# The load of lam in an attention and feed-forward kernel, issued from the Pool queue

## Chip, core and metric

The kernel runs on one core of one Trainium2 chip. The metric is the device time of one execution in microseconds. Before the change it is 221.66 us, the median of twelve runs, which lie between 219.85 and 223.47.

The engines are named as in the profile: PE is the matrix engine (TensorE), ACT is ScalarE, DVE is VectorE, POOL is GpSimd, and SP is SyncE, which here only issues transfers. A transfer (DMA) is issued by SP, ACT or POOL; each of these has a queue of its own for it, and all transfers are carried out by the same 16 DMA engines of the core.

## The reference

For 4 batches, 8 heads, 768 positions and a head size of 64, a linear attention with a decay `lam` for each head is followed by a feed-forward layer. The attention works in blocks of 64 positions:

```python
Dmask = np.where(rel >= 0, lam[:, None, None] ** rel[None, :, :], 0.0)
lam_pow = lam[:, None, None] ** (pos[None, :, None] + 1)
for b in range(nb):
    intra = einsum('bhic,bhjc->bhij', qb, kb) * Dmask[None]
    intra = einsum('bhij,bhjd->bhid', intra, vb)
    inter = einsum('bhid,bhde->bhie', qb * lam_pow[None], kv_state)
    out[:, :, sl] = intra + inter
    kv_state = lam_block * kv_state + einsum('bhsd,bhse->bhde', kb * rev_pow, vb)
```

Its output, as 3072 tokens of 512 values, goes through `x @ w_in` (512 by 2048), a smooth ReLU, which is 0 below -1, h above 1 and (h + 1)^2 / 4 between, and `g @ w_out` (2048 by 512). `lam` has eight values, one for each head; every other number of the attention is scaled by powers of them.

## The kernel before

**Tiles.** The 3072 tokens are 24 blocks of 128 (c = 0 to 23, six of them to a batch). Four blocks are a stage of 512 tokens for the feed-forward layer, so that there are six stages. The matrices of the layer, `w_in_sb` and `w_out_sb`, are loaded once in four pieces each, by POOL (L188, L192), and kept.

**How lam is used.** Instead of a decay in each product, q and k are scaled by tables of powers of lam before anything else. `lam_b` (L106) is a tile of 128 rows in each of which the eight values stand; it is loaded by one transfer that reads the same 32 bytes for each row (L107). ACT takes its logarithm (`ln_lam`, L144), DVE multiplies it with the positions (`arg`, L146), and ACT makes three tables by exponentials: `tab_q` (L149), `tab_p` (L151) and `tab_k` (L154). The positions come from two iotas on POOL (L113, L114) and a copy on ACT (L140).

**A block.** q of two blocks is loaded as `x0f` (L585), k as `x1f` and v as `x2f` (L597); for the first two blocks k and v come together as `raw` (L592). All these loads are issued by SP, in an order that the planner sets. The scaled q is `qs` (L296), on DVE or POOL; the scaled k is `ks` (L287). PE transposes both through PSUM (`py`, L332, and `pt`, L325), ACT copies q's result to `qT` (L338), DVE copies k's to `kT` (L342) or `kbd` (L335). PE multiplies them (`ps`), DVE masks the scores (`sc`, L405 to L410), PE makes the state (`pu`) and the output (`po`), and ACT copies the output to `xT` (L458). From `xT` on the feed-forward layer takes over: PE with `w_in_sb` into `ph` (L470), ACT and DVE for the smooth ReLU (L479 to L500), PE with `w_out_sb` into `py` (L518), ACT to the output tile (L523), SP to memory.

**Setup on POOL.** Before its first `qs`, POOL makes an identity for the transposes, the two iotas, the causal masks (L116 to L126) and clears two of the four tiles `vi` (L138). DVE clears other tiles (L134 to L142) in the same time, and ACT loads its function table (L105).

**Order.** The setup stands in program order on each engine. All that follows is set by a planner, `run_plan` (L217): every operation has an engine, an estimated time, the operations it needs and a time when it is due, and a small simulation of five engines and the transfers decides the order on each engine. Its only guess at the start of the transfers is `FIRST_BYTE` (L212), the time in ns at which the first load is taken to begin.

**First loads.** SP issues the first q (c = 0 and 1), raw k, raw v, k for c = 2, the second q, v for c = 2, k and v for c = 3. POOL issues the first piece of `w_in` after k for c = 2 has landed, and the other three after the second q has been scaled.

Of the kernel before, what the change touches and what calls it, by code (L numbers as in the profile page):

```python
# [23 lines left out]
def kernel(  # L24
# [16 lines left out]
    nc = tc.nc  # L41
# [62 lines left out]

    nc.scalar.preload_act_table_set("natural_log_exp_and_others")  # L105
    lam_b = const.tile([128, H], F32)  # L106
    nc.scalar.dma_start(out=lam_b, in_=lam.partition_broadcast(128))  # L107


    ident = const.tile([128, 128], BF16)  # L110
# [7 lines left out]
        out=causal, in_=causal, compare_op=AX.is_ge, fill=0.0,  # L118
# [3 lines left out]
    for e in range(2):  # L122
        for rows, base in ((slice(0, 128), 128 - e), (slice(0, 64), -e)):
            nc.gpsimd.affine_select(
                out=causal2[rows, e], in_=causal2[rows, e], compare_op=AX.is_ge, fill=0.0,
# [15 lines left out]
    for t in kbd[2:] + ubd[1:]:  # L141
# [10 lines left out]
                         in_=arg[:, 1].rearrange("p (e m) h -> p e (m h)", e=2)[:, :, :2 * H], func=AF.Exp, scale=-1.0)  # L152
# [56 lines left out]
        ops.append(OPS[key])  # L209

    MMS, FETCH = {"s": 8, "o": 12}, 1300
    FIRST_BYTE = 2950  # L212
    LDD, QXD, KXD, STD = 20000, 7000, 7000, 3000
    ON_POOL, ON_DVE = (1,), ((0, 1),)
    W_AFTER = {1: ("cq", 1, 1), 2: ("cq", 1, 1)}
# [1 line left out]
    def run_plan(free):  # L217
# [21 lines left out]
        for x in topo:  # L239
            if not x.needs:  # L240
                ready[x.eng].append((0, x))
        out_seq, xfer, dma_free, fetched = [], [0] * RING, FIRST_BYTE, 0
        while len(out_seq) < len(ops):
# [548 lines left out]
```

## Time and profile before

| | |
|---|---|
| median of twelve runs | 221.66 us |
| the profiled execution's own time | 222.71 us |
| its span on the core | 221.0 us |
| granted clock of PE | 1.00 |
| first matmul starts | 9.41 us |
| lam: issued, from ACT's queue; ln_lam starts | 0.84 us; 6.78 us |
| first q: issued by SP; first qs starts on DVE, on POOL | 0.81 us; 7.76 us, 7.80 us |
| raw k: issued by SP; first ks starts on DVE, on POOL | 1.32 us; 9.56 us, 9.60 us |
| first w_in piece issued by POOL | 12.40 us |
| last matmul ends | about 217.9 us |

The page gives for each engine the time in which it was busy, the chain of work that ended last, and groups of like instructions. Times in the views count from the start of the span. A releaser, what ended an engine's idle time, is inferred from semaphore events. For a transfer the profile gives the time of its issue on the queue and the time from issue to landing, and for each stretch the number of packets that each queue moved: q1 is SP's, q10 is ACT's, q0 is POOL's.

### The profile page before, as it was taken

To read this page: it belongs to the slowest core of one execution; us is meant where nothing else is said; L and a number is where in the kernel's file an instruction comes from. 1 tells how busy PE (TensorE), PEld (TensorE's weight loads), DVE (VectorE), ACT (ScalarE), POOL (GpSimd) and SP (SyncE) were. 2 spreads that over 40 slices of the span, in tenths; PEclk is the share of its full clock that TensorE was granted. 3 is DMA by queue.
4 is the path that set the end of the run, shared out by engine and by line. 5 is a ranking of instruction groups with operands and counts; after the bars stand their busy time and mean duration, and the time that the engine had idled before them with its cause. 6 is when DMAs were issued, how large, how long until landed. Compare 5 with 4: busy or idle time off the path is not lost.

```text
span 221.0 us, 4453 instructions
## 1 busy us (share of the span) xinstructions
PE 203.3 (92%) x1776; PEld 132.8 (60%) x1800; DVE 141.6 (64%) x216; ACT 123.0 (56%) x220; POOL 64.1 (29%) x71
## 2 busy tenths in 40 slices
PE   0189889999999999999999999999999999999994
PEld 0158778686847977777667776654545444444443
DVE  5275859689581888897876866740697745554301
ACT  2247668646646767486757667645665544445030
POOL 8563066217534162733240730332100000000000
PEclk9999999999999999999999999999999999999999
DMA  3999999999999898959999926998985211110122
GB/s 91 254 224 203 178 219 167 177 204 204 176 201 214 177 223 164 249 106 232 195 245 160 260 72 140 203 207 184 293 138 173 47 47 50 47 47 0 50 95 95
DMA packets 96116, 35.42 MB, mean 160 GB/s; under 512 B 78560, under 2 KB 93152, under 8 KB 96096
## 3 DMA queue, kind: packets, MB, share of 16 engines
q1 hardware_dynamic: 91728, 30.94, 66.8%
q0 software_dynamic: 4224, 4.19, 12.0%
q8 instruction: 14, 0.23, 0.4%
q14 instruction: 6, 0.05, 0.1%
q10 hardware_dynamic: 144, 0.00, 0.0%
HBM read 27.27 MB, written 6.29 MB: 152 GB/s over the span
## 4 chain that ended last, share of the span: by engine, by line
PE 90%; DMA 3%; ACT 2%; DVE 2%; issue 1%; POOL 1%; DVEq 0%
PE ph L470 38%; PE py L518 36%; PE ps L398 3%; DMA lam_b<-in_lam_dram 3%; PE po L428 3%; PE pu L369 2%; PE py L512 1%; PE po L425 1%; PE py L332 1%; PE pt L325 1%; PE po L420 1%; ACT xT L458 1%; PE po L446 1%; PE po L417 1%; POOL qs L296 1%
## 5 line engine op out<-in xcount | busy, mean ns | idle before, releaser
L470 PE MATMUL ph<-xT,w_in_sb 128*128 128x256 bf16 (+2 forms) x763 | 95.7, 272 | 1.7 <-ACT xT L458 1.2
L479 ACT ACTIVATE r<-ph,one 128x512 bf16<-128x512 f32 x96 | 65.9, 688 | 48.7 <-PE ph L470 31.8
L518 PE MATMUL py<-w_out_sb,gT 128*128 128x512 bf16 x349 | 86.5, 379 | 1.2 <-issue 0.3
L470 PEld LDWEIGHTS <-w_in_sb 128*128 128x128 bf16 x768 | 63.3, 98 | 24.7 <-issue 1.9
L518 PEld LDWEIGHTS <-gT 128*128 128x128 bf16 x368 | 34.8, 98 | 34.9
L489 DVE TENSOR_SCALAR t<-r 128x1024 bf16<-128x1024 bf16 x48 | 25.1, 524 | 36.6 <-ACT r L479 36.6
L500 DVE TENSOR_TENSOR gT<-w,t 128x1024 bf16<-128x1024 bf16 x48 | 39.6, 825 | 1.5
L495 DVE TENSOR_TENSOR w<-r,t 128x1024 bf16<-128x1024 bf16 x48 | 38.3, 798 | 1.5
L287 POOL TENSOR_TENSOR ks<-x1f,tab_k 128x512 bf16<-128x512 f32 x20 | 23.0, 1149 | 32.0 <-DMA x1f<-in_k_dram 15.6
L296 POOL TENSOR_TENSOR qs<-x0f,tab_q 128x512 bf16<-128x512 f32 x15 | 19.0, 1282 | 17.5 <-PE ph L470 6.0
L523 ACT COPY osb<-py 128x512 f32<-128x512 f32 x23 | 13.5, 585 | 17.9 <-PE py L518 16.6
L373 ACT CAST ubd<-pu 64x256 bf16<-64x256 f32 x40 | 14.6, 364 | 7.4 <-PE pu L369 3.7
L294 POOL TENSOR_TENSOR qs<-x0f,tab_qn 128x512 bf16<-128x512 f32 x8 | 9.7, 1212 | 27.3 <-DMA x0f<-in_q_dram 22.6
L410 DVE TENSOR_TENSOR sc<-ps,causal 128x512 bf16<-128x512 f32 x12 | 8.3, 689 | 9.6 <-PE pt L398 9.6
L458 ACT CAST xT<-po 128x512 bf16<-128x512 f32 x15 | 8.8, 584 | 8.3 <-PE po L428 5.1
L332 PE MATMUL py<-ident,qs 128*128 128x128 bf16 x16 | 2.4, 306 | 10.1 <-POOL qs L296 9.4
L428 PE MATMUL po<-sc,vi 128*128 128x128 bf16 x112 | 10.5, 219 | 0.0
L428 PEld LDWEIGHTS <-vi 128*128 128x128 bf16 x112 | 8.4, 98 | 1.0
L332 PEld LDWEIGHTS <-qs 128*128 128x128 bf16 x24 | 2.1, 121 | 11.0 <-POOL qs L296 9.4
L425 PE MATMUL po<-qT,ubd 128*128 128x128 bf16 x48 | 8.7, 219 | 0.0
L410 DVE TENSOR_TENSOR sc<-ps,causal_n 128x512 bf16<-128x512 f32 x8 | 5.5, 686 | 4.8 <-PE pt L398 4.8
L320 ACT CAST vi<-x2f 128x512 bf16<-128x512 f32 x14 | 8.5, 616 | 0.0
(84 smaller groups left out, 138.7 us busy)
## 6 DMA issues: line engine op xcount, KB each, us to landing
out_dram<-osb SPq DMA_DIRECT2D x23, 256.0 KB, 2.6
x1f<-in_k_dram SPq DMA_DIRECT2D x22, 256.0 KB, 4.9
x2f<-in_v_dram SPq DMA_DIRECT2D x22, 256.0 KB, 4.8
x0f<-in_q_dram SPq DMA_DIRECT2D x8, 512.0 KB, 5.0
w_in_sb<-in_moe_w_in_dram POOLq DMA_DIRECT2D x4, 512.0 KB, 8.7
w_out_sb<-in_moe_w_out_dram POOLq DMA_DIRECT2D x4, 512.0 KB, 9.0
x0f<-in_q_dram SPq DMA_DIRECT2D x8, 256.0 KB, 4.0
raw<-in_k_dram SPq DMA_DIRECT2D x1, 512.0 KB, 8.1
```

The costliest lines, as they stand in the source:

```text
L287: eng.tensor_tensor(ks[c], qkv_ld[c, 1], _bc(tab, 2, D), op=AX.mult)
L296: eng.tensor_tensor(qs[m, e], qkv_ld[m, 0][:, :, e], _bc(tab_q[:, e, m % (NCB // 2), :], 2, D), op=AX.mult)
L373: nc.scalar.copy(out=ubd[c % NUB][HD[hi], :, HD[hi]], in_=pu[0][HD[hi], :, HD[hi]])
L410: nc.vector.tensor_tensor(sc_sb[c][:, g], pst[c, g], _bc(causal if c < DX else causal_n, 1, HP), op=AX.mult)
L428: nc.tensor.matmul(po[:, hp], lhsT=vi[c % NV][:, hp, hi].rearrange("p a d -> p (a d)"), rhs=sc_sb[c][:, hi, hp, :], start=(cb == 0 and hi ...
L470: nc.tensor.matmul(ph[:, j * m:(j + 1) * m], lhsT=w_in_sb[:, ko, (ni + j) * 128:(ni + j + 1) * 128], rhs=xT[s][:, ko, tok], start=(ko == 0 ...
L479: nc.scalar.activation(out=o, in_=x, func=AF.Relu, bias=one[:, 0:1])
L489: nc.vector.tensor_scalar(t, r, 0.5, 1.0, op0=AX.mult, op1=AX.min)
L495: nc.vector.tensor_tensor(w, r, t, op=AX.subtract)
L500: nc.vector.tensor_tensor(gT[s][:, f - RW * n:f, tok].rearrange("p (a b) m -> p a b m", a=RW), w.rearrange("p a (b m) -> p a b m", m=m), t ...
L518: nc.tensor.matmul(py_t[s, ms], lhsT=gT[s][:, ko, ms * 128:(ms + 1) * 128], rhs=w_out_sb[:, ko, :], start=(ko == 0), stop=(ko == FO - 1))
L523: nc.scalar.copy(out=osb[s, ms], in_=py_t[s, ms])
```

## The change

One line issues lam's load from POOL instead of ACT, at the same place in the program, and the planner's guess at the first load's start is 500 ns lower.

```diff
     nc.scalar.preload_act_table_set("natural_log_exp_and_others")
     lam_b = const.tile([128, H], F32)
-    nc.scalar.dma_start(out=lam_b, in_=lam.partition_broadcast(128))
+    nc.gpsimd.dma_start(out=lam_b, in_=lam.partition_broadcast(128))
...
     MMS, FETCH = {"s": 8, "o": 12}, 1300
-    FIRST_BYTE = 2950
+    FIRST_BYTE = 2450
```

## Prediction

> **What bounds the kernel now.** I read the page first: its span, its engine shares and the chain that ended last.
>
> ```profile
> span 221.0 us, 4453 instructions
> PE 203.3 (92%) x1776; PEld 132.8 (60%) x1800; DVE 141.6 (64%) x216; ACT 123.0 (56%) x220; POOL 64.1 (29%) x71
> PE 90%; DMA 3%; ACT 2%; DVE 2%; issue 1%; POOL 1%; DVEq 0%
> ```
>
> TensorE is busy for 203.3 of 221.0 us. The table of busy time by stretch tells where its idle time is (columns: stretch, length, then busy time and instruction count of each engine).
>
> ```profile
> 0.00:9.40 9.40, 0.00 (x0) 0.00 (x0) 4.25 (x11) 2.19 (x6) 6.03 (x18) 1.00 0.68 177
> 9.40:29.30 19.90, 16.56 (x196) 13.69 (x197) 12.06 (x20) 11.59 (x24) 7.21 (x7) 1.00 1.05 193
> 29.30:216.80 187.50, 185.75 (x1565) 118.25 (x1589) 124.44 (x183) 109.19 (x191) 50.90 (x46) 1.00 0.79 158
> ```
>
> Up to 9.40 us TensorE does nothing; then it is 83% busy (16.56 of 19.90); from 29.30 on it idles only 1.75 of 187.50 us. So a shift of the first matmul reaches the end nearly one for one, if the stretch from 9.4 to 29.3 passes it on. The head of the chain, in order of time, is where the change acts (start, length, what).
>
> ```profile
> 0.84 5.92 DMA lam_b<-in_lam_dram
> 6.76 0.02 issue
> 6.78 0.22 ACT ln_lam L144
> ...
> 7.03 0.27 DVE arg L146
> ...
> 7.32 0.24 ACT tab_q L149
> ...
> 7.82 1.54 POOL qs L296
> ...
> 9.41 0.62 PE py L332 x4
> ```
>
> This seems to say that lam's load sets the first matmul. I doubt it. qs needs tab_q, ready at 7.32 + 0.24 = 7.56, and also q's first tile x0f. The view of line L296 shows the wait for x0f as an instruction of its own, ahead of the multiplication; the list of DMA issues gives both landings.
>
> ```profile
> L296 POOLq EVENT_SEMAPHORE  x1: 17/17/17, 7.7 to 7.7; - x1
> x0f<-in_q_dram SPq DMA_DIRECT2D x1, 512.0 KB, 6.8
> lam_b<-in_lam_dram ACTq DMA_DIRECT2D x1, 4.0 KB, 5.9
> ```
>
> x0f is issued at 0.81 and lands 6.8 later, at about 7.6; the wait ends at 7.7 and qs starts at 7.8. For the next cast, ks at L287, the same view has its wait for raw k end at 9.5 and its multiplication start at 9.6, with tables that are two microseconds old by then. The same 0.1 us in both says that x0f's landing, not the tables, released qs. The page infers its releaser; lam is ready some 0.1 us before it is needed. So an earlier lam alone is worth nothing; x0f has to land earlier, or lam later, for the time to move.
>
> **The change, part by part.** Built, both kernels have the same instructions in the same order on every engine except for one row: lam's DMA leaves ScalarE's list and stands in POOL's, after the start barrier and ahead of the identity's memset. So the second edit, FIRST_BYTE 2950 to 2450, moves nothing: 0 us. Semaphore lanes are renumbered. One wait goes (v's load for c = 3 waited for the first q load, landed at 7.6, and issues at 11.92: 0 us); the last w_out load now waits for lam's lane, done some 30 us before: 0 us.
>
> *ScalarE loses an issue* of 0.42 us at 0.84. It ran beside the table load (0.81 to 2.09), and ScalarE then idles 4.5 us until lam: 0 us.
>
> *POOL gains an issue.* The POOL rows of the trace are four w_in issues of 747 to 929 ns, the first being the longest; lam's 4 KB in 128 rows may cost less. I take 0.93. Everything behind it on POOL moves by that: identity, two iotas, two causal masks, two memsets of vi. They end at 5.44 and would end at 6.4; POOL then idles until 7.8 (2.37 us before qs), so it is hidden. Should qs start earlier than 6.4 the cover is gone and each further us costs one. ScalarE's cast of pos_i would start at about 2.4 instead of 2.10, well ahead of lam. Nothing on SP's queue moves in order.
>
> *When does lam land from POOL?* The trace has no small load from there, so bounds. Its issue runs from 0.80 to 1.7. The first w_in issue ended at 13.33 and its queue's first packets came between 14.2 and 14.7, so 0.9 to 1.4 later: lam's first packet at 2.6 to 3.1. From below, w_in(0)'s 528 packets took from there to its landing at 12.40 + 7.5 = 19.9, at most 5.7 us; lam's 144 packets at that rate are 1.6: landing from 4.2 on. From above, lam itself took 6.76 − 2.5 = 4.3 from its first packet on the ScalarE queue: landing by 7.4. I take 5, nearer to the rows of the software queue that it will use. ln, arg and tab_q take 0.80 after it (6.76 to 7.56), so that lam may land up to 6.85 without touching a qs at 7.8. At 5 it costs 0; at 7.4 it costs 0.55.
>
> The Trainium skill, "DMA: Bandwidth & Descriptors", section "Specifications", speaks against the change: it gives about 1 us to the first byte by the GpSimd path and 0.6 by SyncE and ScalarE. By that alone lam would land 0.4 later, at 7.16, and the kernel would lose 0.3 us. No row here shows it.
>
> *What the other loads gain.* This decides. The DMA view by stretch counts packets by queue; q1 is SP's, q10 is lam's.
>
> ```profile
> q1 hardware_dynamic: 164, 0.08, 61.0%
> q10 hardware_dynamic: 4, 0.00, 0.5%
> ...
> q1 hardware_dynamic: 344, 0.18, 48.9%
> q10 hardware_dynamic: 91, 0.00, 3.0%
> ```
>
> The first pair is 2.5 to 3.0 us, the second 3.0 to 4.5. Before lam's packets SP's queue moved 164 per half us and was rising. While 91 of lam's 144 pass, it moves 344 in three halves, 115 each, and the engines are half idle (48.9%). It climbs again to 981 in the three halves from 5.5 to 7.0, with 8 lam packets left. So lam's packets stand where SP's queue falters, and x0f is the load in flight. Had SP's queue kept 164, it would have moved 492: 148 more, which at 164 per half us is 0.45 us. Had it run at 327 from 3.0 to 5.5 it would have moved 1635 instead of 733 (344, and 155 and 234 in the two halves after 4.5): 902 packets, 1.4 us at 327. If lam's packets disturb in the same way from another queue, or the dip is the start of HBM reads and not lam, it is 0. A loss in this term is excluded, since the same 144 packets are served either way. I take 0.45, the rate that the queue had shown by then; ends 0 and 1.4.
>
> *Does the stretch to 29.3 pass it on?* qs, tq, qT and the second tq follow one another; the key transpose at 11.07 needs ks, whose load raw k landed at 9.4 (ks done at 10.25), so 0.45 passes even if raw k stays. Next: ks for c = 2 needs x1f, landed 12.1, used 13.91 (1.8 spare); w_in(0) lands 19.9, used 22.46 (2.5 spare); x2f for c = 3 lands 20.5, used 22.17 (1.6 spare); w_in(1) lands 16.29 + 7.9 = 24.2, used about 25.3 (1.1 spare). So 0.45 passes whole; over 1.1 passes only as far as these loads come earlier too.
>
> **The sum.** ScalarE 0, POOL 0, lam's lateness 0, SP's loads −0.45. Against the profiled execution: span 221.0 − 0.45 = 220.55, and with the 1.71 us around it (222.71 − 221.0) 222.26. That execution is 1.05 above the median of the twelve runs, 221.66, so the median forecast is 221.66 − 0.45 = 221.2. About 0.5%, 1.1 us, is what a measurement of this kernel can tell from no change.
>
> **Rivals.**
> *The transfer is hidden anyway.* The dip belongs to the start of the loads, x0f lands at 7.6 as before: 221.7. For it: 65 packets only in the half us from 2.0 to 2.5, before any of lam's. Against it: the fall after 3.0 comes with lam's packets.
> *The whole dip is lam's.* SP's queue runs on at 327 and x0f lands 1.4 earlier, raw k and the rest with it: 220.3. For it: the recovery follows the end of lam's packets; a 512 KB q load takes a median of 5.0 to land later on, against 6.8 here. Against it: loads before 3.0 were slow without lam, and the tables would have to be ready at 6.2, so lam landed by 5.4.
> *Slower: descriptors made on POOL come late, lam takes x0f's place as the last releaser.* The place is ScalarE's wait at L144; it decides from a landing after 6.85, one for one, since ln, arg, tables, qs and the first matmul queue behind it. Price: like w_in's quickest load, 7.5, landing would be at 8.3, 1.45 late: 223.1; like their median, 8.7, 2.65 late: 224.3. DVE's memsets fill 0.88 to 4.49, beside the issue; would POOL be held until they end, the first packet would come at 5.4 to 5.9 and lam, 1.6 to 4.3 later, at 7.0 to 10.2. Against it: POOL's two memsets of vi, one beside DVE's memsets and one after them, show 944/944/944 ns, so DVE's memsets didn't hold that one; and w_in carries 128 times lam's bytes.
> The Trainium skill, "SBUF — State Buffer", section "SBUF: two separate sides", warns of this: while VectorE runs an operation in a two-port mode, GpSimd can't write descriptors. Memset isn't named there; if it counted, lam would be held as above, and the time be 221.8 to 225.0.
>
> **How the numbers follow.** Chances: forecast 0.40, hidden anyway 0.14, whole dip 0.26, late lam 0.20. The first two lie within 0.5% of before (0.54), the third is faster by over 0.5%, the fourth slower by over 0.5%. The predicted time is the first's, 221.2. Its own range, from 0.55 for a lam at 7.4 to −1.1 for what the spare of w_in(1) passes, is 220.5 to 222.2. The range of 8 in 10 reaches to 220.0, just past the third, and to 223.1, the cheapest end of the fourth.
>
> **What would show it.** Right: lam lands between 4 and 6.5; x0f within 0.2 to 0.8 earlier than 7.6; ScalarE's wait at L144 shrinks and L296 starts on x0f's landing; the first matmul comes at about 9.0 and the idle time after 29.3 stays near 1.75. Wrong: x0f lands at 7.6 as before, and the first matmul stays at 9.4; or L296 waits again for the tables, lam landing after 6.85; or the first matmul moves and TensorE's idle time between 9.4 and 29.3 takes it back, most likely at the second w_in group.

## The result, and the profile after

| | before | after |
|---|---|---|
| median, us | 221.67 (49 runs, 219.85 to 223.47) | 222.56 (12 runs, 222.14 to 223.25) |
| profiled execution, us (its span) | 222.71 (221.0) | 222.24 (220.5) |

The ratio of after to before is 1.0047, with a 95% interval from 1.0026 to 1.0067: so after is slower, by 0.9 us between the medians. The two profiled executions alone would say the opposite, since that of before was a slow one of its kind; this is taken up below. VectorE, ScalarE and POOL run the same instructions in the same order in both traces, but for lam's issue, so the planner's lower guess has moved nothing and the difference is lam's queue.

The start of after in order of time (start, length, engine, line, operation; in brackets the idle time before it and what ended it):

```profile
1.34 0.71 POOL L107 DMA_DIRECT2D lam_b<-in_lam_dram  x1 [0.83 <-POOLq L776]
...
7.21 0.21 ACT L144 ACTIVATE ln_lam<-lam_b 128x8 f32<-128x8 f32 x1 [4.16 <-DMA lam_b<-in_lam_dram]
...
7.75 0.24 ACT L149 ACTIVATE tab_q<-arg 128x48 f32<-128x48 f32 x1 [0.33 <-DVE arg L146]
...
8.02 0.69 DVE L296 TENSOR_TENSOR qs<-x0f,tab_q 128x512 bf16<-128x512 f32 x1 [0.31 <-ACT tab_q L149]
8.07 1.54 POOL L296 TENSOR_TENSOR qs<-x0f,tab_q 128x512 bf16<-128x512 f32 x1 [1.37 <-ACT tab_q L149]
8.63 1.53 DVE L287 TENSOR_TENSOR ks<-raw,tab_p 128x512 bf16<-128x512 f32 x1
...
9.67 0.61 PE L332 MATMUL py<-ident,qs 128*128 128x128 bf16 x4 [9.67 <-POOL qs L296]
```

Its first DMA issues, with microseconds from issue to landing:

```profile
x0f<-in_q_dram SPq DMA_DIRECT2D x1, 512.0 KB, 4.3
raw<-in_k_dram SPq DMA_DIRECT2D x1, 512.0 KB, 6.7
lam_b<-in_lam_dram POOLq DMA_DIRECT2D x1, 4.0 KB, 5.8
```

x0f now lands at 0.81 + 4.3 = 5.1 instead of 7.6. But lam lands at 1.34 + 5.8 = 7.15, and qs starts at 8.02 and 8.07 on the tables, three microseconds after its data came. The packets of the queues say why x0f gained (first 3.0 to 4.5 us, then 4.5 to 6.5):

```profile
q1 hardware_dynamic: 997, 0.50, 111.5%
...
q1 hardware_dynamic: 738, 0.37, 75.6%
q0 software_dynamic: 27, 0.00, 28.4%
```

SP's queue moves 997 packets from 3.0 to 4.5, where it moved 344 before; the dip has gone with lam and stands now at 4.5 to 6.5, where 27 of lam's packets, 32 on this queue, are served. Behind the start TensorE's idle time is nearly as before, 2.01 against 1.75 us (last columns: clock, DMA share, GB/s):

```profile
29.30:216.80 187.50, 185.49 (x1568) 118.00 (x1590) 124.71 (x184) 108.58 (x190) 48.63 (x44) 1.00 0.73 154
```

### The profile page after: what moved, and what is told of

Its sections match the earlier page's. It is cut to its first block, busy times and chain, and to the rows that moved or that the text cites. A ratio compares the mean times of both kernels' runs of the same rounds, so it can differ in the third digit from the quotient of the medians.

```text
span 220.5 us, 4453 instructions
## 1 busy us (share of the span) xinstructions
PE 202.5 (92%) x1776; PEld 131.9 (60%) x1800; DVE 142.4 (65%) x216; ACT 122.8 (56%) x220; POOL 63.9 (29%) x72
## 4 chain that ended last, share of the span: by engine, by line
PE 74%; DMA 16%; SPq 5%; POOL 2%; issue 1%; DVE 1%; ACT 0%; DVEq 0%
PE py L518 33%; PE ph L470 30%; DMA w_out_sb<-in_moe_w_out_dram 6%; DMA x0f<-in_q_dram 6%; DMA w_in_sb<-in_moe_w_in_dram 5%; SPq L597 3%; PE ps L398 2%; PE po L428 2%; PE pu L369 2%; PE py L512 1%; PE po L425 1%; POOL qs L296 1%; SPq L592 1%; PE po L420 1%; PE po L417 1%
## 5 line engine op out<-in xcount | busy, mean ns | idle before, releaser
L495 DVE TENSOR_TENSOR w<-r,t 128x1024 bf16<-128x1024 bf16 x48 | 39.1, 814 | 1.5
L287 POOL TENSOR_TENSOR ks<-x1f,tab_k 128x512 bf16<-128x512 f32 x20 | 24.9, 1247 | 27.5 <-DMA x1f<-in_k_dram 13.0
L296 POOL TENSOR_TENSOR qs<-x0f,tab_q 128x512 bf16<-128x512 f32 x15 | 17.1, 1158 | 19.4 <-DMA x0f<-in_q_dram 12.1
L294 POOL TENSOR_TENSOR qs<-x0f,tab_qn 128x512 bf16<-128x512 f32 x8 | 9.0, 1122 | 31.7 <-DMA x0f<-in_q_dram 27.8
```

The costliest lines, as they stand in the source:

```text
L287: eng.tensor_tensor(ks[c], qkv_ld[c, 1], _bc(tab, 2, D), op=AX.mult)
L296: eng.tensor_tensor(qs[m, e], qkv_ld[m, 0][:, :, e], _bc(tab_q[:, e, m % (NCB // 2), :], 2, D), op=AX.mult)
L495: nc.vector.tensor_tensor(w, r, t, op=AX.subtract)
```

## The experiments

**Both kernels again.** Three more executions of before and one of after were profiled.

> The kernel before, unchanged, profiled a second time. Theory A (late lam): the change is slower because lam, issued from POOL, lands at 7.15 us and the tables are ready at 7.99, so the first matmul comes at 9.67; the profiled execution of before was a slow one of its kind (222.71 against a median of 221.67), and in a usual one the first matmul comes sooner: at 8.4 to 8.9 for a time near 221.7. Theory B (later loss): the start isn't the cause; the first matmul of before comes at 9.3 to 9.5 whatever the time, and the 0.9 us are lost after it, by POOL's or the transfers' later order.

> The kernel before, unchanged, profiled a third time. Theory A: time minus first matmul is the same constant within 0.5 us in all profiled executions of before (213.3 in the first), and lam's landing differs between them. Theory B: the first matmul is the same within 0.3 us in all of them, and the difference in time lies behind it.

> The kernel before, profiled a fourth time. Theory G (a race of two queues, issued 30 ns apart): one of the two outcomes again, and nothing between: lam's first packet at about 1.9, landing at 4.5, x0f at 6.2, first matmul at 8.0, time 219.7 to 221; or lam's first packet at about 3.0, landing at 6.8, x0f at 7.7, first matmul at 9.4, time 222 to 223.

> The kernel after, unchanged, profiled a second time. Theory A: lam's first packet comes again at 4.5 to 5.2 and lands at 7.0 to 7.3, the first matmul at 9.5 to 9.8, the time 222.1 to 223.0. Theory B: the start may vary by more than that without the time following.

| execution | us | lam's first packet | lam lands | x0f lands | first matmul on qs | us minus first matmul |
|---|---|---|---|---|---|---|
| before, first | 222.71 | 2.96 | 6.76 | 7.66 | 9.41 | 213.30 |
| bef2 | 220.54 | 1.86 | 4.53 | 6.26 | 8.01 | 212.53 |
| bef3 | 219.75 | 1.86 | 4.46 | 6.23 | 7.98 | 211.77 |
| bef4 | 221.88 | 2.28 | 6.17 | 7.85 | 9.60 | 212.28 |
| after, first | 222.24 | 4.87 | 7.19 | 5.12 | 9.67 | 212.57 |
| aft2 | 222.78 | 4.64 | 7.11 | 5.02 | 9.59 | 213.19 |

Here is bef3's list of issues, to be read beside the one above:

```profile
x0f<-in_q_dram SPq DMA_DIRECT2D x1, 512.0 KB, 5.4
...
lam_b<-in_lam_dram ACTq DMA_DIRECT2D x1, 4.0 KB, 3.6
```

So before starts in more than one way. SP's and ScalarE's issues stand 30 ns apart; in two executions of four x0f lands at 6.2 to 6.3 and the first matmul comes at 8.0, in two at 7.7 to 7.9 and 9.4 to 9.6. bef4 is a third way, which theory G didn't expect: lam's packets first, but both late. Both executions of after start at 9.6 to 9.7. Theory A holds in that before can start earlier (earlier even than its 8.4 to 8.9), but its constant doesn't: the last column differs by 1.5 us, so something is lost or won behind the first matmul too. The time behind it can be cut in three, at the first product into `po` and at the first product with `w_in_sb`; beside them stands the time of ks for c = 2:

| execution | ks for c = 2 | first matmul to first po | first po to first product with w_in_sb | what is left |
|---|---|---|---|---|
| before, first | 1.53 | 8.56 | 4.49 | 200.25 |
| bef2 | 0.68 | 7.93 | 4.33 | 200.27 |
| bef3 | 0.68 | 7.94 | 3.60 | 200.23 |
| bef4 | 1.46 | 8.49 | 3.55 | 200.24 |
| after, first | 1.29 | 8.33 | 3.55 | 200.69 |
| aft2 | 1.34 | 8.37 | 4.48 | 200.34 |

So two causes make nearly all of the 1.5 us. (The 0.4 us more that is left in the first execution of after is not explained.) The first are VectorE's and POOL's multiplications. First bef3, then after:

```profile
12.49 0.68 DVE L287 TENSOR_TENSOR ks<-x1f,tab_k 128x512 bf16<-128x512 f32 x1
...
12.99 2.08 POOL L296 TENSOR_TENSOR qs<-x0f,tab_q 128x512 bf16<-128x512 f32 x2 [0.72 <-DMA x0f<-in_q_dram]
```

```profile
14.18 1.29 DVE L287 TENSOR_TENSOR ks<-x1f,tab_k 128x512 bf16<-128x512 f32 x1
...
12.88 2.04 POOL L296 TENSOR_TENSOR qs<-x0f,tab_q 128x512 bf16<-128x512 f32 x2 [0.79 <-DMA x0f<-in_q_dram]
```

The same ks takes 0.68 us when POOL's qs starts after it, and 1.29 when POOL's is under way. In all fourteen profiles of this study it takes 0.68 without and 1.29 to 1.53 with such a meeting. POOL's start is set by the second q's landing, ks by the chain from the first matmul. They meet in both late executions of before and in both of after; ks is then 0.6 to 0.85 us longer, and the first po comes 0.4 to 0.6 us later. The second cause, in the column from the first po to `w_in_sb`, is TensorE's own speed; it is told at the end.

So the loss can be placed. The two late executions of before (222.71 and 221.88) lie on average within 0.3 us of the two of after (222.24 and 222.78); the two early ones (220.54 and 219.75) lie 2.4 below these. What the change takes away is the early start, which before has in a part of its executions. An estimate from these means and from the means of all runs (221.63 and 222.62) puts that part at about a third; it wasn't counted.

**No lam at all.**

```diff
-    nc.gpsimd.dma_start(out=lam_b, in_=lam.partition_broadcast(128))
+    nc.vector.memset(lam_b, 0.98)
```

> The kernel after without the load of lam: VectorE fills lam_b with 0.98, so that all heads decay alike. Theory A: with no lam to wait for, qs starts on x0f's landing at about 5.1 to 5.3, the first matmul at 6.8 to 7.1, and the time is 2.2 to 2.9 below after, about 219.9. Theory B: the first matmul may come sooner, but the time stays within 0.7 of after.

219.31 us, 0.9919 of before (0.9891 to 0.9947). x0f lands at 4.95 and the first matmul comes at 6.70. Theory A holds in kind, and each of its numbers is passed a little on the early side. Waiting for lam is worth 3.2 us to after by the medians, and 1.8 to before by the ratio, whose runs were taken beside these. x0f, at 4.95 here and 5.1 in after, also shows that POOL's lam leaves it nearly alone; the load behind it, raw k, lands at 6.76 here and at 8.0 in after.

**What makes POOL's lam late.** First VectorE's memsets (0.88 to 4.49) were moved:

```diff
-    nc.vector.memset(one, 1.0)
-    for t in vi[:2] + kbd[:2] + ubd[:1]:
-        nc.vector.memset(t, 0.0)
...
                             _bc(ln_lam, 1, 2 * NCB), op=AX.mult)
+    nc.vector.memset(one, 1.0)
+    for t in vi[:2] + kbd[:2] + ubd[:1]:
+        nc.vector.memset(t, 0.0)
```

(the second group of memsets goes with them)

> The kernel after, with VectorE's setup memsets (0.88 to 4.49 us) moved behind arg, so that VectorE is silent while POOL's transfer of lam is made. Theory C (VectorE holds POOL's descriptors): lam's first packet, at 4.64 and 4.87 in two executions of after, waits for the memsets' end; now it comes at 2.6 to 3.3 and lam lands at 4.8 to 5.6. Theory D (the POOL queue's own start): the first packet comes again at 4.6 to 4.9, 2.6 to 2.9 behind the issue's end, and lam lands at 7.0 to 7.3. The time is not the point, since VectorE's first qs now waits behind 3.5 us of memsets: 222 to 225.

With VectorE silent (its first instruction, then lam's issue and landing) lam's first packet comes at 5.01 and lam lands at 7.22: theory C falls.

```profile
7.48 0.26 DVE L141 TENSOR_TENSOR arg<-pos,ln_lam 128x96 f32<-128x96 f32 x1 [7.48 <-ACT ln_lam L139]
...
lam_b<-in_lam_dram POOLq DMA_DIRECT2D x1, 4.0 KB, 5.9
```

The time was 223.29 in one run. Then SP's loads were held until lam had landed:

```diff
+        if c == 0 and x == 0:
+            tc.add_manual_dep(d.ins, lam_d.ins.name, SYNC)
```

> The kernel after, with SP's first load, and so all of SP's queue, held until lam has landed. Theory D1 (POOL's path is slow to start by itself): lam's first packet comes at 4.6 to 5.0 although no other transfer runs, and lam lands at 5.2 to 6.5. Theory D2 (lam waits behind SP's transfers on the 16 DMA engines): with these idle its first packet comes at 2.3 to 3.0 and it lands by 3.5. The time is not the point: all loads start after lam, 3 to 5 us later than in after.

With the DMA engines otherwise idle the first packet comes at 2.75 (list of issues, then packets from 2.5 to 3.0):

```profile
lam_b<-in_lam_dram POOLq DMA_DIRECT2D x1, 4.0 KB, 2.9
...
q0 software_dynamic: 6, 0.00, 24.6%
```

lam lands at 4.23, less early than D2 expected, but 2.9 earlier than in after: D2 holds for the first packet, D1 falls (and theory C once more, since VectorE's memsets ran from 0.88 to 4.49 here). In after lam's packets wait while SP's 512 KB for x0f are served (they appear at 4.6 to 4.9, x0f lands at 5.0 to 5.1) and then share the engines with raw k. Of the 5.8 us from issue to landing these two make 2.9: the first packet comes 2.1 later (4.87 against 2.75), and from there to the landing it takes 2.3 instead of 1.5. On ScalarE's queue lam didn't wait for the whole of x0f: in the first profile of before its packets came from 2.96 on, and x0f landed at 7.66. The time, 223.05 in one run, holds SP's late start.

**One row instead of 128**, spread by TensorE; from ScalarE's queue, and from POOL's:

```diff
+    lam_1 = const.tile([1, H], F32)
+    nc.scalar.dma_start(out=lam_1, in_=lam.partition_broadcast(1))
+    ones_1 = const.tile([1, 128], F32)
+    nc.vector.memset(ones_1, 1.0)
+    lam_b = pp_u.tile([128, H], F32, name="lam_b", tag="pu")
+    nc.tensor.matmul(lam_b, lhsT=ones_1, rhs=lam_1, start=True, stop=True)
```

> The kernel before, with lam loaded once, as one row of 32 bytes, from ScalarE's queue; TensorE spreads it over 128 rows by a product with a column of ones, and ScalarE reads the result from PSUM. Theory E (the 128 rows are the cost, whatever the queue): lam lands by 3.5, SP's queue shows no dip, x0f lands at 4.9 to 5.3, the first matmul on qs comes at 6.7 to 7.3, and the time is that of the kernel without lam, 219.0 to 220.0. Theory F (the queue is the cost): the time stays within 0.7 of before, 220.6 to 221.8.

> The same single row, from POOL's queue. Theory E with D: the first packet still comes at 4.5 to 4.9, but lam lands at once, at 5.0 to 5.6 instead of 7.1; the tables are ready at 6.1 to 6.7, the first matmul on qs comes at 7.8 to 8.5, and the time is 1.0 to 1.8 below after: 220.8 to 221.6. Theory F: lam lands at 6.5 to 7.3 as in after, and the time is 222.2 to 223.0.

From ScalarE 218.66 us, 0.9903 of before (0.9872 to 0.9934). Its start:

```profile
0.83 0.52 ACTq L107 DMA_DIRECT2D lam<-in_lam_dram  x1
...
2.15 0.56 PE L111 MATMUL lam_b<-lam,ones 1*128 1x8 f32 x2 [2.15 <-DMA lam<-in_lam_dram]
2.75 0.18 ACT L148 ACTIVATE ln_lam<-lam_b 128x8 f32<-128x8 f32 x1 [0.45 <-PE lam_b L111]
...
5.06 0.69 DVE L300 TENSOR_TENSOR qs<-x0f,tab_q 128x512 bf16<-128x512 f32 x1 [0.36 <-ACT tab_q L153]
```

lam is used at 2.15, x0f lands at 4.96 and the first matmul on qs comes at 6.71. Theory E holds on this queue (the time is even 0.3 below its range), and this version beats both kernels. From POOL it is 222.29 us, 1.0046 of before (1.0029 to 1.0063), where 220.8 to 221.6 was expected: a single row, its first packet at 4.80, lands at 6.22, and with 0.6 for TensorE's step the tables are only 0.3 earlier than in after. So neither theory stands alone: 128 rows cost about 0.9 to 1.0 of POOL's landing (7.11 and 7.19 against 6.22), and what keeps it late is the place in the line. A single row is no single packet there: POOL's queue moves 32 packets for it, as many as for 128 rows, where ScalarE's moves 2. This run also limits what was said of the meeting: its first matmul is as late as 9.38, but ks takes 0.68, since the second q lands at 11.69, 1.1 earlier than in after, and POOL's qs is over when ks starts. A late start alone doesn't make them meet.

**lam on SP's own queue**, ahead of q and right behind it:

```diff
+    nc.sync.dma_start(out=lam_b, in_=lam.partition_broadcast(128))
```

> lam in 128 rows, but from SP's queue, ahead of the first q. In two of three executions of before lam's packets came first (from 1.86 us), lam landed at 4.5 and x0f at 6.25; in the third x0f's came first (1.95 against 2.96), lam landed at 6.76 and x0f at 7.66. Theory G (a race of two queues decides, and lam first is the better outcome): one queue makes lam always first: it lands at 4.0 to 4.8, x0f at 6.2 to 6.9 (0.45 later issued), the first matmul at 8.0 to 8.6, the time 219.8 to 221.0 with less spread than before. Rival: the order in the queues isn't what decides; x0f lands at 7 to 7.8 and the time is at or over that of before.

> lam in 128 rows from SP's queue, right behind the first q. Theory G: this is the worse outcome of the race made certain: x0f lands at 4.9 to 5.4 since nothing goes ahead of it, but lam only after it, at 5.3 to 6.9; tables 0.8 later, first matmul at 7.8 to 9.3, so slower than with lam first (219.36). Rival: the order on the queue doesn't matter, lam lands by 4.5 and the time is within 0.4 of lam first.

Ahead of q, and then behind it (issues, then ks and POOL's qs):

```profile
x0f<-in_q_dram SPq DMA_DIRECT2D x1, 512.0 KB, 4.5
...
lam_b<-in_lam_dram SPq DMA_DIRECT2D x1, 4.0 KB, 2.9
...
12.00 0.68 DVE L287 TENSOR_TENSOR ks<-x1f,tab_k 128x512 bf16<-128x512 f32 x1
...
12.52 2.07 POOL L296 TENSOR_TENSOR qs<-x0f,tab_q 128x512 bf16<-128x512 f32 x2 [0.72 <-DMA x0f<-in_q_dram]
```

```profile
x0f<-in_q_dram SPq DMA_DIRECT2D x1, 512.0 KB, 4.1
...
lam_b<-in_lam_dram SPq DMA_DIRECT2D x1, 4.0 KB, 4.5
...
12.79 1.48 DVE L290 TENSOR_TENSOR ks<-x1f,tab_k 128x512 bf16<-128x512 f32 x1
...
12.68 2.49 POOL L299 TENSOR_TENSOR qs<-x0f,tab_q 128x512 bf16<-128x512 f32 x2 [0.68 <-DMA x0f<-in_q_dram]
```

Ahead of q: lam lands at 3.75, x0f at 5.75, the first matmul comes at 7.50, and the time is 219.36, 0.9925 of before (0.9903 to 0.9947), better than expected, with runs from 219.20 to 219.96. Behind q: x0f at 4.96, lam at 5.80, the first matmul at 8.28, and 221.54, 0.9998 of before (0.9969 to 1.0026). Theory G holds in that lam's place in the line decides. Of the 2.2 us between the two, 0.8 is the first matmul; ks takes 0.68 in the first and 1.48 in the second, which puts the first po 0.6 further behind the first matmul.

**Other rows.** 128 different rows in place of one:

```diff
+    nc.sync.dma_start(out=lam_b, in_=q[0, 0, 0:128, 0:H])
...
-    nc.scalar.activation(out=ln_lam, in_=lam_b, func=AF.Ln)
+    nc.scalar.activation(out=ln_lam, in_=lam_b, func=AF.Ln, scale=0.0, bias=one[:, 0:1])
```

> lam first on SP's queue, but with 128 different rows of 32 bytes (from q) in place of the one row read 128 times; the logarithm takes a constant instead, so all decays are 1 and the output is another. Theory H1 (reading one address 128 times is what makes the rows dear): they land by 3.2 instead of 3.75, and x0f by 5.5 instead of 5.75. Theory H2 (small rows are dear wherever they come from): landings within 0.2 of 3.75 and 5.75.

They land at 2.60 instead of 3.75, and x0f at 5.75 as with lam: H1 is right for the rows themselves, H2 for what goes after them. One run took 220.53.

## Why the prediction was wrong

- *What released qs in the profile of before.* Right: x0f, not lam, and bef2 and bef3 show it more plainly (lam at 4.5, x0f at 6.2).
- *The base.* Wrong, and about half of the miss. The sum was made against one execution whose first matmul came at 9.41, and carried to a median 1.05 us lower as if that were noise. It wasn't noise alone: two of four executions of before start at 8.0, and a late lam takes that start away.
- *ScalarE's issue and POOL's issue.* Right: 0 on the path; POOL's took 0.71, not 0.93, but began at 1.34 instead of 0.80. POOL was free before qs, 1.37 us in after.
- *When lam lands from POOL: "I take 5", cost 0.* This step failed. It landed at 7.11 to 7.19, near the upper bound of 7.4, so that the first matmul came at 9.67, where the sum has 9.41 − 0.45 = 8.96. That is 0.7 of the 1.4 us between the forecast of 221.2 and the result; the base is the rest. The first packet was put at 2.6 to 3.1, from w_in's delay; it came at 4.6 to 4.9. With idle engines it comes at 2.75, so the delay of the path was sized right and the wait behind SP's loads was left out. Nor does POOL's queue move the 144 packets that the working counts on, but 32.
- *SP's loads: −0.45.* The mechanism was right, the size too small: x0f came 2.5 earlier than in that profile, beyond the term's end of 1.4, and 1.1 earlier than in bef2 and bef3. It was worth nothing, because the tables took its place as the last releaser; with no lam, or one row from ScalarE, it paid.
- *The stretch up to 29.3.* The list of spares held landings only; the meeting of ks with POOL's qs wasn't in it, and cost 0.4 to 0.6 us on the path where it happened. The first profile of before has it too, so against that profile it cost nothing.
- *The rivals.* The late lam was the right one in place (L296 waited for the tables, as its sign said), and the whole dip in kind, since x0f gained even more than its 1.4. The late lam's ground was not the right one: it looked to descriptors made late on POOL, and the wait was behind SP's loads. By its threshold of 6.85 a landing at 7.15 costs 0.3 against the first profile, and the first matmul moved from 9.41 to 9.67, by 0.26. Its price from w_in's loads, 1.45 or more, was too high.
- *The rules of the Trainium skill.* "DMA: Bandwidth & Descriptors", section "Specifications", gives the GpSimd path 0.4 us more to the first byte: with idle engines POOL's first packet came 1.4 after its issue, that of ScalarE's single row 0.9, a difference of 0.5, so this agrees; it is not what made lam late. "SBUF — State Buffer", section "SBUF: two separate sides", didn't apply: with the memsets away lam's first packet still came at 5.01.

What isn't settled: how the two queues' race in before falls one way or the other. Four profiles show three ways; how often each comes wasn't measured. Nor does any run tell what sets the time of TensorE's step, below.

## What to carry to other kernels

A small load that all else waits for belongs at the head of the queue that carries the big loads (219.36 here), or in a form that needs one row (218.66 from ScalarE); from POOL's queue its packets came behind the 512 KB that the DMA engines already had, with one row too (222.29). Look for the last releaser and the one just before it: a gain on the first is worth no more than the distance to the second. When runs of one kernel lie 1.6% apart, as here, one profile is not a base: profile it several times before a microsecond is counted.

## What the hardware showed unexpectedly

- TensorE doubles its rate in mid-run, and not at a fixed time. From the timeline of bef3:

```profile
16.96 0.30 PE L446 MATMUL po<-sc,vi 64*128 64x128 bf16 x1
...
17.07 0.25 PE L446 MATMUL po<-sc,vi 64*128 64x128 bf16 x1
...
17.16 0.22 PE L446 MATMUL po<-sc,vi 64*128 64x128 bf16 x1
...
17.21 0.22 PE L446 MATMUL po<-sc,vi 64*128 64x128 bf16 x1
```

Matmuls 0.11 us apart become 0.05 apart, while the granted clock's row reads 1.00 throughout. (The trace's own records of that clock begin only with the step, at 17.12 here and at 21.51 in the first profile of before; 1.00 ahead of it is no measurement.) The first fast matmul comes at 17.2 here, 18.8 in bef2, 19.2 in bef4, 21.5 in the first profile of before, 19.1 and 21.5 in the two of after. This explains the stretch from the first po to `w_in_sb` in the second table above: where the step comes 1.1 to 1.3 us after the first po, the stretch takes 3.55 to 3.60; where it comes 2.9 after, 4.33; where 3.5 after, 4.48 to 4.49. The Trainium skill, "TensorE: Matmul & The Clock Gate", section "Part 1: The HAM clock gate (the "warmup" mystery)", tells of half the clock until about 3.4 us of activity, counted in a free-running window, so that it varies from run to run; the halving and the variation agree. The 3.4 us can't be checked here, since the first matmuls have gaps between them: the step comes 9.2 to 12.1 us after the first one.
- VectorE's product of two SBUF tiles takes about twice as long beside one of POOL's that started first (0.68 against 1.29 to 1.53). "SBUF — State Buffer", section "Who interferes with whom", has it so for a VectorE instruction with two SBUF inputs and a GpSimd one that reads SBUF; the runs agree.
- Reading one row of 32 bytes 128 times took 1.15 us longer to land than reading 128 different rows (3.75 against 2.60, one profile of each).
